# From the sixth group on, q and k come as bf16 blocks by casting DMA and are transposed by DMA

## The chip, the cores and the metric

The kernel runs on one core of one Trainium2 chip. Its time is device time in microseconds; three runs of the kernel before gave 258.83, 259.00 and 259.49 us, a median of 259.0. The profile is of one further execution, whose own time was 260.0 us and whose span from the first to the last instruction was 258.2 us. The TensorE clock was granted in full (1.0).

## The reference

Two layers, one after the other. First block-causal attention over 8 batches, 8 heads, 576 positions and head size 64, in fp32:

```python
scores = scale * np.matmul(q, k.transpose(0, 1, 3, 2))      # scale = 1/8
mask = (pos[:, None] // 64) >= (pos[None, :] // 64)
attn = softmax(np.where(mask, scores, -1e9))
attn_out = np.matmul(attn, v)
```

Then the heads are laid side by side as x, 4608 tokens of 512 features, and go through a maxout layer with 1024 hidden features:

```python
g = np.maximum(x @ w1, x @ w2)
out = g @ w_out
```

## The kernel before, in words

**Algebra of the second layer.** max(a, b) is b + max(a - b, 0). The kernel forms d = w1 - w2 once, computes relu(x d) (`h_unit`, line 202; the relu is line 220) and adds x (w2 w_out) with M = w2 w_out computed once (`m_unit`). An output tile of 128 tokens (`y_unit`, line 252) is 4 matmuls of x with M and 8 of g with w_out.

**Tiling of the attention.** Two heads make a pair, since two heads of 64 fill the 128 partitions; two pairs make a group g. There are 32 pairs and 16 groups (NG), two groups (GPB) to a batch. Everything is computed in transposed form: the scores matmul (`scores`, line 366) needs q and k with the head dimension on the partitions (tiles `qT` and `kT`, one per pair, a ring of four, NT = 4), and so does the second layer with x (`xT`).

**How q and k get there before the change.** `load_qk(g, ...)` (line 112) loads a group's q and k, fp32, by two DMAs on SP's queue into raw tiles (three buffers each; position 9p + t of a head goes to partition p, so that each partition reads one run of 2304 bytes per head). A tiny memset on Pool ahead of each (`gated`) keeps the load from starting too early. `cast` (line 126) turns them into bf16 on Pool, one instruction of 1152 values per partition each. `transposes` (line 346) transposes them on TensorE, 18 matmuls with the identity per q or k of a group into two PSUM tiles, and copies these into `qT` and `kT`, one on DVE, one on ACT (line 360). v is loaded by Pool's casting DMA (`load_v`, line 134), five chunks per batch.

**Softmax and attention times v.** For each pair three PSUM tiles of scores are filled (`tile_0`, `tile_1`, `tile_2`), ACT takes the exponential into `aT` (`exp`, line 395), and Pool zeroes the blocks above the diagonal (`mask`, line 400). `tile_2` has corner blocks whose keys come from `kz`, a copy of some columns of `kT` made on Pool by `pad_keys` (line 377). `av` (line 463), two pairs later (LAG = 2), multiplies with v on TensorE, and DVE divides by the row sums into `xp`.

**x.** For the first four groups and the last, TensorE transposes `xp` into `xT` (`x_out`). For groups 4 to 14 SP does it with two transposing DMAs (`x_dma`, lines 494 to 497), one group later than the scores.

**Order of the work.** The order is written out by hand (`manual_schedule`): each engine executes its instructions in the order in which the Python code emits them. The second layer is a list of units, from which `fill(n)` emits some n matmuls wherever attention would leave TensorE waiting; a unit may be emitted once the tokens it reads are accounted done (`done_tokens`). In the main loop each group of two pairs a and b emits: the scores of a's first two tiles; for a, then for b: fill, `av` of two pairs ago, for b also `x_dma` of the group before, then the transposes of the next group's q (at a) or k (at b) by `t_pair`, further score tiles, the copies out of the transposes, the exps and masks, at b also `pad_keys` for the next group, and last `pool_work` (line 541), which holds Pool's share: loads for the group three ahead, casts for the group two ahead, v for the next batch. SP's queue holds the loads of q and k, the transposes of x and the stores of y, in the order emitted; a store waits there until ACT or DVE has copied its tile out of PSUM.

Of the kernel before, what the change touches and what calls it, by code (L numbers as in the profile page):

```python
# [9 lines left out]
BF16 = mybir.dt.bfloat16  # L10
# [4 lines left out]
def kernel(  # L15
# [10 lines left out]
    nc = tc.nc  # L26

    B, H, S, D = q.shape
    P = 128
    BLK = 64  # L30
# [14 lines left out]
    NG = NPAIR // 2  # L45
    GPB = HP // 2
# [36 lines left out]
    raw = ctx.enter_context(tc.tile_pool(name="raw", bufs=3))  # L83
# [10 lines left out]
    NV, NA, NT = 3, 4, 4  # L94
    qT_r = [ring.tile([P, S], BF16, name=f"qT{r}") for r in range(NT)]
    kz_r = [ring.tile([P, 3 * BLK], BF16, name=f"kz{r}") for r in range(NT)]
    kT_r = [ring.tile([P, S], BF16, name=f"kT{r}") for r in range(NT)]
# [12 lines left out]
    dve, pool, act = nc.vector.tensor_copy, nc.gpsimd.tensor_copy, nc.scalar.copy  # L110

    def load_qk(g, queues, gated=False):
        b, u = divmod(g, GPB)
        for nm, src, queue in (("q", q, queues[0]), ("k", k, queues[1])):
            if queue is None:
                continue
            raws[nm, g] = t = raw.tile([P, 2, RPP * D], FP32, name=f"{nm}raw")
            if gated:
                nc.gpsimd.memset(t[:, 0, :1], 0.0)
            queue.dma_start(  # L120
                out=t[:],
                in_=src[b, 4 * u:4 * u + 4].rearrange(
                    "(s h) (p t) d -> (h p) s (t d)", h=2, t=RPP),
            )

    def cast(nm, g, parts):
        t = raws[nm, g].rearrange("p s (t d) -> p t s d", d=D)
        if (nm, g) not in qk_n:
            qk_n[nm, g] = qkn.tile([P, RPP, 2, D], BF16, name=f"{nm}n")
        n = qk_n[nm, g]  # L130
        for copy, j0, j1 in parts:
            copy(out=n[:, j0:j1], in_=t[:, j0:j1])  # L132

    def load_v(b, c):
        rows = min(P, S - c * P)
        nc.gpsimd.dma_start(  # L136
            out=vv_r[b % NV][P - rows:, c, :, :D],
            in_=v[b, :, c * P:c * P + rows, :].rearrange("h p d -> p h d"),
        )
# [7 lines left out]
    for j in range(d_ff // WB):  # L147
        row, n = (1, j) if j < 3 else (3, 0)
# [22 lines left out]
    dve, pool, act = nc.vector.tensor_copy, nc.gpsimd.tensor_copy, nc.scalar.copy  # L171
# [174 lines left out]
    def transposes(nm, g, copies):  # L346
        n = qk_n.pop((nm, g))
        pts = [ps_m.tile([P, RPP, NP], BF16, name=f"ps_{nm}T", tag="m") for _ in range(2)]
        for j in range(RPP):
            for i in range(2):  # L350
                r = slice(i * NP, (i + 1) * NP)
                nc.tensor.transpose(  # L352
                    pts[i][:, j, :], n[r, j].rearrange("p s d -> p (s d)"), ident[r, r],
                )

        def copy_out(which=(0, 1), part=(0, NP), copy=None):
            p0, p1 = part
            for i in which:
                t = (qT_r if nm == "q" else kT_r)[(2 * g + i) % NT]
                (copy or copies[i])(  # L360
                    out=t[:, p0 * RPP:p1 * RPP].rearrange("q (p j) -> q p j", j=RPP),
                    in_=pts[i][:, :, p0:p1].rearrange("q j p -> q p j"),
                )
        return copy_out
# [67 lines left out]
    def tile_0(p):  # L432
        u = ps_s.tile([P, 2, 512], FP32, name="ps_s", tag="s")
        scores(p, u, 0, 0, 0, 512)
        return lambda: (exp(p, u, 512, 0), mask(p, 0))

    def tile_1(p):
        u = ps_s.tile([P, 2, 512], FP32, name="ps_s", tag="s")
        scores(p, u, 0, 0, 512, 64)
        scores(p, u, 64, 1, 128, 448)  # L440
        return lambda: (exp(p, u, 512, 512), mask(p, 576))

    def tile_2(p):
        u = ps_s.tile([P, 2, 512], FP32, name="ps_s", tag="s")
        corner_scores(p, u, 320)
        scores(p, u, 0, 2, 256, 320)
        scores(p, u, 384, 3, 448, P)

        def out():
            exp(p, u, 512, 1024)  # L450
            nc.scalar.activation(
                out=aT_r[p % NA][BLK:, :, 1536:AW], in_=u[BLK:, :, 320:320 + BLK],
                func=AF.Exp, scale=scale,
            )
            mask(p, 1024)
            mask(p, 1344)
        return out

    def region(*tiles):
        for out in tiles:  # L460
            out()
# [29 lines left out]
    def x_by_dma(g):  # L491
        return BY_DMA <= g < NG - 1

    def x_dma(g):
        b, u = divmod(g, GPB)
        for s in range(2):
            nc.sync.dma_start_transpose(
                out=xT[:, 2 * u + s, b * S:b * S + NCH * P].rearrange(
                    "p (t w) -> p t w", w=P),
                in_=xps[g][:, s].rearrange("p t a d -> p (t a d)"),  # L500
            )

    def x_out(g, t0=0, t1=NCH, copies=(dve, dve)):
        b, u = divmod(g, GPB)
        if x_by_dma(g):
            if u == GPB - 1:
                done_tokens[0] = (b + 1) * S
            return
        xp = xps[g]
        n = t1 - t0  # L510
        n_odd = min(t1, NCH - 1) - t0
        pe = ps_m.tile([P, 2, n, BLK], BF16, name="ps_xe", tag="m")
        po = ps_m.tile([P, 2, n_odd, BLK], BF16, name="ps_xo", tag="m")
        for s in range(2):
            for t in range(t0, t1):
                src = xp[:, s, t].rearrange("p a d -> p (a d)")
                nc.tensor.transpose(pe[:, s, t - t0, :], src[:BLK], ident[:BLK, :BLK])
                if t < NCH - 1:
                    nc.tensor.transpose(po[:, s, t - t0, :], src[BLK:], ident[BLK:, BLK:])
        dst = xT[:, 2 * u:2 * u + 2, b * S + t0 * P:b * S + t1 * P].rearrange(  # L520
            "p s (t h w) -> p s t h w", h=2, w=BLK)
        copies[0](out=dst[:, :, :, 0], in_=pe[:])
        copies[1](out=dst[:, :, :n_odd, 1], in_=po[:])
        if u == GPB - 1:
            done_tokens[0] = min(b * S + t1 * P, (b + 1) * S)
# [8 lines left out]
    def fill_of(g):  # L534
        if g == NG - 1:
            return 45
        left = 5 - g if g < 5 else 2 - (g - 5) % 2
        return -(-max(0, ready() - KEEP) // left)


    def pool_work(s):
        g, i = divmod(s, 2)
        if s == 4:
            load_qk(4, (SP, SP), gated=True)
        elif s == 5:
            load_qk(5, (SP, SP), gated=True)
            cast("q", 4, ((pool, 0, RPP),))
            cast("k", 4, ((pool, 0, RPP),))
        else:
            if i == 1 and g + 3 < NG:  # L550
                load_qk(g + 3, (SP, SP), gated=True)
            if i == 1 and g + 2 < NG:
                cast("q", g + 2, ((pool, 0, RPP),))
                cast("k", g + 2, ((pool, 0, RPP),))
            nb, j = divmod(s + 2, HP)
            if nb < B:
                for c in ((0, 1), (2, 3), (4,), ())[j]:
                    load_v(nb, c)

    T_AT = {s: [("qk"[s % 2], s // 2 + 1)] for s in range(NPAIR - 2)}  # L560
    T_AT[0] = T_AT[1] = T_AT[2] = T_AT[3] = []

    def t_pair(s):
        outs = [transposes(nm, g, (dve, act)) for nm, g in T_AT.get(s, [])]
        return lambda: [f() for f in outs]


# [3 lines left out]
    def av_with(p, n):  # L571
        av(p, [0, 1])
        fill(n)
        av(p, [2, 3, 4])
# [82 lines left out]
    outs = tile_0(4), tile_1(4)  # L657
# [13 lines left out]
    n = fill_of(GPB)  # L671
# [10 lines left out]
    for g in range(GPB + 1, NG):  # L682
        a, b = 2 * g, 2 * g + 1
        old = done_tokens[0]
        if x_due:
            x_out(x_due.pop())
        n, new = fill_of(g), done_tokens[0]
        region(tile_0(a), tile_1(a))
        lo, hi = max(3, n // 18), n * 2 // 9
        for p, tiles in ((a, lambda: (tile_2(a), tile_0(b))), (b, lambda: (tile_1(b), tile_2(b)))):  # L690
            if p == a and x_by_dma(g - 2):
                done_tokens[0] = old
            rest = fill(hi)
            done_tokens[0] = new
            fill(rest)
            av_with(p - LAG, lo)
            if p % 2 and x_by_dma(g - 1):
                x_dma(g - 1)
            copy_out = t_pair(p)
            outs = tiles()  # L700
            copy_out()
            region(*outs)
            if p % 2 and g + 1 < NG:
                pad_keys(p + 1)
                pad_keys(p + 2)
            pool_work(p)
        x_due.append(g - 1)
        fill(n - 2 * (lo + hi))
# [49 lines left out]
```

The softmax here doesn't subtract the row's maximum and nothing guards it: scores larger than these inputs give would overflow.

## Time and profile before

| | |
|---|---|
| median of three runs | 259.0 us |
| profiled execution | 260.0 us, span 258.2 us |
| TensorE (PE) busy | 247.4 us, 96% |
| weight loads (PEld) | 139.1 us, 54% |
| VectorE (DVE) busy | 136.1 us, 53% |
| ScalarE (ACT) busy | 143.2 us, 55% |
| Pool (GpSimd) busy | 110.4 us, 43% |
| transposes of q and k on TensorE (L352) | 2 x 288 matmuls, 7.0 and 7.1 us busy |
| casts of q and k on Pool (L132) | 1.15 us each |
| copies of qT and kT out of PSUM (L360) | 0.64 us on ACT, 0.75 us on DVE each |
| v loads' issue on Pool (L136) | 40 of them, mean 0.85 us |
| transposes of x, issue on SP (L497) | 22 of them, median 1.27 us |

PE is TensorE, PEld its weight loads, DVE VectorE, ACT ScalarE, POOL GpSimd and SP SyncE, which here only issues DMAs. L352 is line 352 of the kernel. Issuing a DMA is not counted as busy, so the time that Pool spends on the v loads stands beside its 43%. DMA packets are listed by queue: q1 is SP's, q0 Pool's; the share given with them adds the packets' own durations, which overlap. Besides the page, the trace's records of single DMA packets (queue, size, start, duration) can be counted in a stretch of time. "Group" in what follows is one round of the main loop.

### The profile page before, as it was taken

The numbers are of one execution on the slowest core, as the hardware profiler recorded it, in microseconds if no ns is written. First come the engines' busy times: TensorE is split into PE (matmuls) and PEld (weight loads), VectorE is DVE, ScalarE is ACT, GpSimd is POOL, SyncE is SP. The second block draws the span as 40 slices with busy tenths as digits, with TensorE's granted clock in tenths as the row PEclk, the third lists the DMA queues.
The fourth block names the chain that finished last, engine by engine and source line by source line (L and its number), as shares of the span: only waits on it lengthen the run. The fifth ranks groups of instructions, "written<-read, shape, count | busy, mean of one in ns | idle before, by whom it ended". The sixth has DMA issues, their size and how long they took to land.

```text
span 258.2 us, 7195 instructions
## 1 busy us (share of the span) xinstructions
PE 247.4 (96%) x2983; PEld 139.1 (54%) x2983; DVE 136.1 (53%) x299; ACT 143.2 (55%) x200; POOL 110.4 (43%) x274
## 2 busy tenths in 40 slices
PE   7598899799999999999999999999999999999995
PEld 2346678646555555555555554546464655444444
DVE  4967986556584428451845184518550853443200
ACT  2798854476574857586757665766576431000111
POOL 1987950584637263726382638163813010000000
PEclk9999999999999999999999999999999999999999
DMA  6999999499569995998599949985977122202122
GB/s 244 316 206 307 217 251 246 156 102 253 129 162 257 144 188 135 245 154 225 114 244 143 186 145 224 168 196 141 91 109 110 44 56 80 83 0 81 43 104 99
DMA packets 71265, 41.30 MB, mean 160 GB/s; under 512 B 53568, under 2 KB 58048, under 8 KB 71232
## 3 DMA queue, kind: packets, MB, share of 16 engines
q1 hardware_dynamic: 28544, 31.27, 43.4%
q0 software_dynamic: 42272, 8.92, 39.9%
q10 hardware_dynamic: 416, 0.66, 0.7%
q8 instruction: 23, 0.38, 0.6%
q14 instruction: 10, 0.08, 0.1%
HBM read 34.60 MB, written 9.44 MB: 171 GB/s over the span
## 4 chain that ended last, share of the span: by engine, by line
PE 84%; DMA 8%; POOL 3%; ACT 2%; issue 1%; DVE 0%; SPq 0%; POOLq 0%; ACTq 0%
PE ps_y L257 36%; PE ps_h L215 22%; PE ps_o L479 10%; PE ps_s L371 8%; DMA qraw<-in_q_dram 5%; DMA kraw<-in_k_dram 3%; PE ps_qT L352 2%; PE ps_kT L352 2%; PE ps_w L341 1%; ACT aT L395 1%; PE ps_y L272 1%; PE ps_M L238 1%; POOL kn L132 1%; PE ps_s L389 1%; ACT qT L360 1%
## 5 line engine op out<-in xcount | busy, mean ns | idle before, releaser
L395 ACT ACTIVATE aT<-ps_s 128x1024 bf16<-128x1024 f32 (+2 forms) x100 | 95.8, 996 | 25.8 <-PE ps_s L371 24.2
L257 PE MATMUL ps_y<-wo_sb,g 128*128 128x512 bf16 x280 | 69.8, 379 | 0.0
L215 PE MATMUL ps_h<-xT,d_sb 128*128 128x512 bf16 (+3 forms) x320 | 69.2, 358 | 0.3 <-DVE d_sb L162 0.3
L220 DVE TENSOR_SCALAR g<-ps_h 128x512 bf16<-128x512 f32 (+3 forms) x80 | 50.7, 636 | 30.6 <-PE ps_h L215 28.8
L400 POOL MEMSET aT<- 64x128 bf16 x124 | 22.4, 200 | 81.8 <-ACT aT L395 81.2
L485 DVE RECIPROCAL rec<-ps_o 128x4 f32<-128x4 f32 (+1 forms) x64 | 12.1, 188 | 62.5 <-PE ps_o L479 61.7
L215 PEld LDWEIGHTS <-d_sb 128*128 128x128 bf16 x320 | 29.0, 98 | 29.1 <-issue 2.7
L479 PEld LDWEIGHTS <-aT 128*128 128x128 bf16 x960 | 37.2, 98 | 13.5 <-issue 0.8
L262 ACT COPY y<-ps_y 128x512 f32<-128x512 f32 x31 | 18.2, 587 | 44.5 <-PE ps_y L257 36.1
L257 PEld LDWEIGHTS <-g 128*128 128x128 bf16 x280 | 25.8, 98 | 29.8 <-issue 2.0
L479 PE MATMUL ps_o<-vv,aT 128*128 128x65 bf16 x960 | 39.8, 194 | 0.0
L257 PE MATMUL ps_y<-m_sb,xT 128*128 128x512 bf16 x140 | 38.2, 380 | 0.0
L136 POOL DMA_DIRECT2D vv<-in_v_dram x40 | 33.7, 848 | 1.6 <-issue 1.2
L371 PE MATMUL ps_s<-qT,kT 64*128 64x64 bf16 (+6 forms) x344 | 31.2, 280 | 1.6 <-ACT kT L360 0.7
L486 DVE TENSOR_TENSOR xp<-ps_o,rec 128x256 bf16<-128x256 f32 (+1 forms) x64 | 31.4, 491 | 2.2
L360 ACT COPY qT<-ps_qT 128x576 bf16<-128x576 bf16 (+1 forms) x17 | 10.3, 614 | 19.9 <-PE ps_qT L352 19.9
L132 POOL CAST qn<-qraw 128x1152 bf16<-128x1152 f32 (+1 forms) x16 | 16.9, 1058 | 9.1 <-DMA qraw<-in_q_dram 9.1
L257 PEld LDWEIGHTS <-xT 128*128 128x128 bf16 x140 | 12.2, 98 | 15.1 <-issue 3.5
L371 PEld LDWEIGHTS <-kT 64*128 64x128 bf16 x344 | 12.3, 94 | 11.0 <-issue 6.2
L132 POOL CAST kn<-kraw 128x1152 bf16<-128x1152 f32 (+1 forms) x15 | 17.1, 1140 | 1.4 <-DMA kraw<-in_k_dram 1.4
L360 ACT COPY kT<-ps_kT 128x576 bf16<-128x576 bf16 x15 | 9.6, 639 | 14.4 <-PE ps_kT L352 14.4
L207 POOL COPY g<-g 128x512 bf16<-128x512 bf16 x8 | 4.9, 614 | 20.7 <-DVE g L220 20.3
(58 smaller groups left out, 161.8 us busy)
## 6 DMA issues: line engine op xcount, KB each, us to landing
qraw<-in_q_dram SPq DMA_DIRECT2D x16, 576.0 KB, 5.0
out_dram<-y SPq DMA_DIRECT2D x35, 256.0 KB, 3.7
kraw<-in_k_dram SPq DMA_DIRECT2D x15, 576.0 KB, 5.8
vv<-in_v_dram POOLq DMA_DIRECT2D x32, 128.0 KB, 5.7
w1raw<-in_moe_w_dram POOLq DMA_DIRECT2D x4, 512.0 KB, 8.1
xT<-in_moe_w_dram POOLq DMA_DIRECT2D x4, 256.0 KB, 8.6
wo_sb<-in_moe_w_out_dram POOLq DMA_DIRECT2D x2, 512.0 KB, 10.0
kraw<-in_k_dram ACTq DMA_DIRECT2D x1, 576.0 KB, 5.6
```

Of the source, the lines that this page charges most:

```text
L132: copy(out=n[:, j0:j1], in_=t[:, j0:j1])
L136: nc.gpsimd.dma_start(out=vv_r[b % NV][P - rows:, c, :, :D], in_=v[b, :, c * P:c * P + rows, :].rearrange("h p d -> p h d"),)
L215: nc.tensor.matmul(pt[:, :w], d_sb[:, c, f * P:(f + 1) * P], xT[:, c, t0:t0 + w], start=(c == 0), stop=(c == NDM - 1),)
L220: nc.vector.tensor_scalar_max(g[:, f, m:m + w], pt[:, :w], 0.0)
L257: nc.tensor.matmul(py[:], lhs, rhs, start=(n == 0), stop=(n == len(terms) - 1),)
L262: (dve if i < 2 else act)(out=y[:], in_=py[:])
L360: (copy or copies[i])(out=t[:, p0 * RPP:p1 * RPP].rearrange("q (p j) -> q p j", j=RPP), in_=pts[i][:, :, p0:p1].rearrange("q j p -> q p j"),)
L371: nc.tensor.matmul(ps[:, hh, col:col + w], kT[r, k0:k0 + P], qT[r, q0:q0 + w], start=True, stop=True,)
L395: nc.scalar.activation(out=aT_r[p % NA][:, :, a0:a0 + w], in_=ps[:, :, :w], func=AF.Exp, scale=scale,)
L400: (eng or nc.gpsimd).memset(aT_r[p % NA][BLK:, :, a0:a0 + BLK], 0.0)
L479: nc.tensor.matmul(po[:, gi, hh, :], a[:, hh, a0:a0 + P], vv[:, c, h0 + 2 * hh, :], start=(mm == 0), stop=(mm == n_mm - 1),)
L486: nc.vector.tensor_mul(xp[:, :, ts[0]:ts[0] + n, p % 2].rearrange("q s t d -> q t s d"), po[:, :, :, :D], rec[:, :n].to_broadcast([P, n, 2 ...
```

## The change

From group 5 on (the sixth), q and k take another way. `load_blocks` issues eight casting DMAs on Pool's queue per group, one per head of q and of k, each reading a head as nine blocks of 64 positions and writing bf16 into 64 partitions of a tile that shares the raw tiles' buffers. `transpose_blocks` issues four transposing DMAs on SP's queue per group, one per pair of q and of k, straight into `qT` and `kT`. The loads of group g + 2 are emitted by `pool_work` for the first pair of group g, ahead of the v loads; the transposes of group g + 1 are emitted in group g after `av` of the first pair. The fp32 loads on SP, their gating memsets, the casts on Pool, the transposes on TensorE and the copies out of PSUM are left out for these groups. Groups 0 to 4 are as before. The work of the second layer and its order are untouched.

```diff
     def load_qk(g, queues, gated=False):
         b, u = divmod(g, GPB)
         for nm, src, queue in (("q", q, queues[0]), ("k", k, queues[1])):
-            if queue is None:
+            if queue is None or by_dma(nm, g):
                 continue
...
+    T_DMA = {nm: 5 for nm in "qk"}
+    blk_n = {}
+
+    def by_dma(nm, g):
+        return g >= T_DMA.get(nm, NG)
+
+    def load_blocks(nm, g):
+        b, u = divmod(g, GPB)
+        blk_n[nm, g] = n = raw.tile([P, S // BLK, 2, D], BF16, name=f"{nm}b", tag=f"{nm}raw")
+        for h in range(2):
+            for s in range(2):
+                nc.gpsimd.dma_start(
+                    out=n[h * BLK:(h + 1) * BLK, :, s],
+                    in_=(q if nm == "q" else k)[b, 4 * u + 2 * s + h].rearrange(
+                        "(j p) d -> p j d", p=BLK),
+                )
+
+    def transpose_blocks(nm, g):
+        n = blk_n.pop((nm, g))
+        for h in range(2):
+            nc.sync.dma_start_transpose(
+                out=(qT_r if nm == "q" else kT_r)[(2 * g + h) % NT].rearrange(
+                    "q (j p) -> q j p", p=BLK),
+                in_=n[h * BLK:(h + 1) * BLK].rearrange("p j s d -> p (j s d)"),
+            )
+
     def cast(nm, g, parts):
+        if by_dma(nm, g):
+            return
...
             if i == 1 and g + 3 < NG:
                 load_qk(g + 3, (SP, SP), gated=True)
+            if i == 0:
+                for nm in "qk":
+                    if g + 2 < NG and by_dma(nm, g + 2):
+                        load_blocks(nm, g + 2)
             if i == 1 and g + 2 < NG:
                 cast("q", g + 2, ((pool, 0, RPP),))
                 cast("k", g + 2, ((pool, 0, RPP),))
...
-        outs = [transposes(nm, g, (dve, act)) for nm, g in T_AT.get(s, [])]
+        outs = [transposes(nm, g, (dve, act)) for nm, g in T_AT.get(s, []) if not by_dma(nm, g)]
...
             if p % 2 and x_by_dma(g - 1):
                 x_dma(g - 1)
+            if p % 2 == 0:
+                for nm in "qk":
+                    if g + 1 < NG and by_dma(nm, g + 1):
+                        transpose_blocks(nm, g + 1)
             copy_out = t_pair(p)
```

## The prediction

> **What bounds the kernel now.** I read the page first: busy times, then the DMA queues.
>
> ```profile
> span 258.2 us, 7195 instructions
> ...
> PE 247.4 (96%) x2983; PEld 139.1 (54%) x2983; DVE 136.1 (53%) x299; ACT 143.2 (55%) x200; POOL 110.4 (43%) x274
> ...
> q1 hardware_dynamic: 28544, 31.27, 43.4%
> q0 software_dynamic: 42272, 8.92, 39.9%
> ```
>
> TensorE is 96% busy; DVE, ACT and Pool are near half. q1 is SP's queue, q0 is Pool's. Next the chain that ended last, in order of time, over one group of the loop:
>
> ```profile
> 157.64 0.54 PE ps_s L371 x6
> ...
> 161.56 0.37 PE ps_qT L352 x18
> 161.93 0.06 PE ps_s L389 x4
> ...
> 165.80 0.37 PE ps_kT L352 x18
> ...
> 170.63 0.54 PE ps_s L371 x6
> 171.17 1.40 PE ps_y L257 x6
> 172.57 0.43 PE ps_h L215 x2
> ```
>
> Columns are start, us, work. From 58 us on the chain is TensorE alone, and one group takes 170.63 - 157.64 = 12.99 us (13.0 in the others too). The two transposes that the change removes stand on it, 0.37 us each. By the starts of their neighbours they cost a little less: 161.50 to 161.77, 0.28 us.
>
> Since the change moves work onto DMA, I then asked for the DMA rate in four stretches (columns: length; busy us of PE, PEld, DVE, ACT, Pool; clock; DMA share; GB/s):
>
> ```profile
> 37.50:39.20 1.70, 1.70 (x29) 1.22 (x28) 1.54 (x3) 0.64 (x1) 1.06 (x3) 1.00 2.42 154
> 144.00:145.00 1.00, 1.00 (x9) 0.31 (x7) 0.00 (x0) 0.01 (x1) 1.00 (x2) 1.00 1.28 213
> 182.50:184.00 1.50, 1.50 (x12) 0.51 (x9) 1.26 (x2) 0.00 (x0) 1.50 (x4) 1.00 1.62 159
> 157.64:170.63 12.99, 12.99 (x166) 7.04 (x168) 4.35 (x11) 9.32 (x13) 6.59 (x18) 1.00 1.08 198
> ```
>
> A share above 1 says that packets overlap, so it is no measure of fullness; rates are. In the first stretch only Pool's v loads run, from a backlog, in packets of 128 B written: 154 GB/s / 128 B = 1200 packets per us, and the packet records agree (2050 in 1.7 us). In the second SP's transposes of x run nearly alone: 768 packets of 256 B in 1 us. In the third both have a backlog: the records count 470 of Pool's and 632 of SP's in 1.5 us, 735 per us together. Three more such stretches (77.5 to 80.5, 129.5 to 131.5, 155.5 to 158.5) give 714, 746 and 711. So Pool's small packets and SP's transposes together run no faster than transposes alone.
>
> Last, SP's and Pool's own order of time:
>
> ```profile
> 161.32 4.79 SPq L263 DMA_DIRECT2D out_dram<-y  x2
> 166.66 2.53 SPq L497 DMA_TRANSPOSE xT<-xp  x2
> ```
>
> ```profile
> 157.90 1.16 POOL L132 CAST kn<-kraw 128x1152 bf16<-128x1152 f32 x1
> 158.99 1.75 POOL L136 DMA_DIRECT2D vv<-in_v_dram  x2
> ...
> 165.27 0.69 POOL L136 DMA_DIRECT2D vv<-in_v_dram  x1
> ```
>
> **What the Trainium skill says.** "DMA: Bandwidth & Descriptors", section "Issuing engines are not separate DMA queues": DMAs of SP, ACT and Pool run on the same 16 engines and interleave. The mixed stretches agree. Its section "Why small descriptors are slow (HBM only)" puts a fixed overhead on every packet. The trace agrees: q1's load packets of 2304 B take 93 ns at the median, Pool's of 128 B 32 ns, 18 times fewer bytes in a third of the time. "VectorE: DVE Perf Modes", section "The three transpose paths", has 390 ns on TensorE and 1309 ns by DMA for a 128x128 block. In this trace SP spends 1268 ns at the median on a transpose of five such blocks, so I use that.
>
> **The change part by part**, for the eleven groups 5 to 15.
>
> *TensorE.* 22 sets of 18 transposes go: 22 x 0.28 = 6.2 us by starts, 22 x 0.37 = 8.1 by the chain. I take the middle, 7.1; the group becomes about 12.35 us.
>
> *ACT, DVE.* 22 copies each out of PSUM go (0.64 us on ACT, 0.75 on DVE). Neither sets the group, so this is worth nothing by itself; the exps, and so the masks, come some 0.6 us earlier.
>
> *Pool.* The casts (two of 1.15 us) and two gating memsets (0.2) go, 2.5 us per group; eight loads come, each 64 x 9 runs of 64 values, 576 packets. The v load with 512 packets holds Pool 0.69 us, the one with 1024 0.88: I take 0.71, eight are 5.7 us. Net +3.2 us; Pool has 6.4 us idle in the group shown. The loads stand between the masks of a pair's first tiles and those of its last, with the copies into kz behind. Moving the block that began at 152.61 on with its two v loads: 152.6 + 5.7 + 1.75 = 160.1, masks 0.6, kz 0.5: 161.2, against corner scores due at 161.77 less 0.65 for the faster group. With ACT's 0.6 us it just fits. Any added wait on a load (in the built program each Pool DMA waits for the eighth before it) comes through to TensorE there.
>
> *SP.* Two loads (0.4 us each) go, four transposes come. Each reads 576 rows of 256 B where one of x reads 640: 1268 x 576 / 640 = 1.14 us, four 4.6 us. This form is not in the trace; if the cost goes by blocks of 128 columns (nine against five) it is 2.3 us, four 9.1. I take 1.14. Behind them in SP's order stand y's store, and then x's pair.
>
> *DMA engines.* Per group, mean over a batch's two: Pool 8 x 576 = 4608 packets new, v (4 x 1024 + 512) / 2 = 2304 as before; SP 4 x 576 = 2304 new, x 2 x 640 = 1280 as before; y some 256 to 300 packets of 84 ns; the 512 packets of 2304 B go. Priced with the rates above:
> - SP's 3584 transposed packets, mixed, at some 385 per us: 9.3 us, in which about 340 per us of Pool's pass, 3170.
> - Pool's other 3740 at 1200: 3.1 us.
> - y: 295 x 84 / 16 = 1.55 us.
> - Sum 14.0 us. With the isolated rate of Pool's pairs (53 to 56 us: 1989 in 3 us) for the rest it is 16.5; with no mixing, 3584 / 768 + 6912 / 1200 + 1.55 = 12.0.
>
> The same sum for the kernel before: 1280 / 385 = 3.3, the other 1170 of v 1.0, loads 512 x 93 / 16 = 3.0, y 1.55: 8.9 of 13.0 us, hidden with room. After, 14.0 against TensorE's 12.35: the DMA engines set the group.
>
> *What is late next.* Loads are issued a group before their transposes, and these most of a group before the scores, so early lateness is absorbed; then Pool stalls on its eighth-back DMA, with masks and kz behind, or x's pair lands late. Groups 4 to 13 have both parts: 10 x (14.0 - 13.0) = +10; group 14 has only transposes, -0.65. Span 258.2 + 9.4 = 267.6. The profiled execution took 260.0, 1.8 us around its span, and stands 1.0 above the median 259.0; so the median is span + 0.8: **268.4, say 268**.
>
> **The rivals.**
>
> *All hidden, faster.* Transposes and loads start at different times of a group (SP near its fourth us, Pool near its eighth) and mix little. If the mean rate is above (6912 + 3584) / (12.35 - 1.55) = 970 packets per us, between the mixed 725 and the pure 1200, TensorE stays the bound: 258.2 - 7.1 + 0.8 = 252, with a us for leftovers 253. For it: no engine but TensorE is near full. Against: SP is issuing 7.2 of 12.35 us (4.6 and x's 2.6) and Pool's loads stream for most of the group, so they must overlap.
>
> *Only x is late.* When a batch ends, its x pair (issued 166.66, last packet 170.1) is needed by the first ps_h at 172.57, 2.4 us later. After, it runs inside the new burst. Pairs that met v packets landed up to 3.2 us later than clean ones (3.45 us from first issue; 6.6 at the worst). A loss of 1 to 3 us in about four groups takes back 4 to 12 of the 7: 254 to 264, about 259.
>
> *SP or Pool bound.* At 2.3 us per transpose SP issues 9.1 + 2.6 + 1 = 12.7 us per group and x's pair starts some 4 us later than it may; or the loads cost 0.88 us and their waits add up on Pool. 2 to 3 us over 13.0 in ten groups: 278 to 288.
>
> *That it does not do what it says* is excluded: the built program has 792 fewer TensorE rows, 88 casting loads and 44 transposes on SP.
>
> **How the numbers follow.** DMA engines as the bound 0.42 (260 to 284 by itself), all hidden 0.22, only x late 0.18 (of it 0.05 faster, 0.06 same, 0.07 slower), SP or Pool bound 0.18. Within 0.3% is about what a measurement tells from no change. Faster 0.22 + 0.05 = 0.27; same 0.06; slower 0.42 + 0.07 + 0.18 = 0.67. Range 252.5 to 286: it takes in most of the hidden case and the mixed rate down to 15.8 us per group, and leaves out a cleaner success and the upper part of the SP case.
>
> **What would show it.** Right: the start-to-start of groups near 14 us where both parts run; packets near 725 per us for most of the group; kz (L406) or Pool's loads (L137) waiting for DMA, and TensorE idle before scores or ps_h. The TensorE step is right if ps_qT and ps_kT fall from 288 matmuls each to 90; the Pool step if L137 is near 0.71 us; the SP step if L146 is near 1.14. Wrong if groups are 12.4 us and TensorE still 96% busy (hidden), if idle time stands only before the first ps_h of a batch (x late), or if SP or Pool issues without a gap while the DMA rate is low.

## The result and the profile after

The changed kernel took 288.05 us (median of four executions, 286.13 to 289.4) where the kernel before took 259.12 in the same comparison: 1.111 times as long, 95% interval 1.1033 to 1.1187. The forecast was 268 with a range of 252.5 to 286. The sign was right, the size was too small by 20 us, and the time lies above the range. Ratios here and below leave disturbed executions out, so for four kernels (`q_only`, `unread`, `turn_late` and `turn_late_dve`) they lie below the ratio of the medians.

The profiled execution took 289.4 us. Its page, with the busy times, the row of the granted TensorE clock (tenths, 40 slices) and the two DMA queues:

```profile
span 287.6 us, 6494 instructions
...
PE 255.8 (89%) x2587; PEld 138.6 (48%) x2587; DVE 121.8 (42%) x277; ACT 131.3 (46%) x178; POOL 149.8 (52%) x318
...
PEclk9999999999599968999799979997799999999999
...
q0 software_dynamic: 94368, 15.41, 78.2%
q1 hardware_dynamic: 49312, 24.78, 43.0%
```

TensorE has 396 instructions fewer than before (2983 - 2587, the 2 x 198 transposes taken out), and yet is busy 8.4 us longer, because its clock is no longer granted in full. Pool's queue carries 94368 packets instead of 42272, SP's 49312 instead of 28544, for the same bytes (41.25 MB in all, 41.30 before).

In the lines of the changed kernel, L137 is the new loads, L146 the new transposes, L164 the loads of v, L243 the matmuls of x with d, L399 the scores, L406 the copies into `kz`, L507 attention times v and L525 the transposes of x; in the kernels of the experiments they can lie some lines off.

The waits (us in all, times, longest), of TensorE and of Pool's copies into `kz`:

```profile
PE ps_h L243 <- DMA xT<-xp: 13.8, 8, 3.4
...
POOL kz L406 <- DMA kT<-kb: 6.5, 5, 2.6
...
PE ps_s L399 <- DMA kT<-kb: 4.8, 4, 2.2
...
PE ps_o L507 <- DMA vv<-in_v_dram: 3.5, 1, 3.5
```

None of these four waits is in the kernel before. The largest is not for q and k, which the change moved, but for x, which it did not touch. The chain that ended last shows it too (start, us, work):

```profile
159.97 1.29 SPq L525
161.32 6.95 DMA xT<-xp
168.30 1.01 PE ps_h L243 x2
```

In the kernel before this stretch of the chain was TensorE alone. Now it leaves TensorE for SP's issue of x's second transpose and 6.95 us of its transfer.

From the starts of each group's first scores, groups 5 to 14 took 18.67, 12.47, 18.89, 13.31, 18.21, 13.59, 17.95, 14.75, 18.51 and 13.23 us, 15.96 in the mean, against 13.0 before. Ten times 2.96 is 29.6, which is the whole loss of span (287.6 - 258.2 = 29.4). So a short group and a long one take turns, with the two groups of a batch. One such pair, by windows (length; busy us of PE, PEld, DVE, ACT, Pool; clock; DMA share; GB/s), and then two parts of the long group:

```profile
147.80:161.39 13.59, 12.53 (x129) 6.54 (x129) 3.08 (x9) 8.22 (x11) 11.90 (x24) 1.00 1.98 147
161.39:179.34 17.95, 14.04 (x129) 7.38 (x130) 7.64 (x16) 7.01 (x9) 8.02 (x20) 0.90 1.22 150
...
164.01:167.38 3.37, 0.01 (x1) 0.00 (x0) 0.61 (x2) 0.35 (x1) 1.25 (x4) 1.00 1.72 165
167.70:171.10 3.40, 2.86 (x37) 2.00 (x35) 1.08 (x3) 0.00 (x0) 0.00 (x0) 0.50 1.21 282
```

For 3.37 us TensorE does nothing, and then it runs for 3.4 us at a clock of 0.50. The order of time of SP, of Pool and of TensorE (start, us, work; in brackets the idle time before it and what ended it) shows what it waited for:

```profile
152.04 2.92 SPq L146 DMA_TRANSPOSE qT<-qb  x2
155.12 4.13 SPq L146 DMA_TRANSPOSE kT<-kb  x2
159.35 0.52 SPq L291 DMA_DIRECT2D out_dram<-y  x1
159.97 2.72 SPq L525 DMA_TRANSPOSE xT<-xp  x2
```

```profile
155.21 2.93 POOL L137 DMA_DIRECT2D qb<-in_q_dram  x4 [0.32 <-issue]
158.10 2.96 POOL L137 DMA_DIRECT2D kb<-in_k_dram  x4
160.97 0.78 POOL L164 DMA_DIRECT2D vv<-in_v_dram  x1
```

```profile
161.39 0.61 PE L399 MATMUL ps_s<-qT,kT 64*128 64x512 bf16 x6 [1.06 <-DMA kT<-kb]
...
163.67 0.34 PE L507 MATMUL ps_o<-vv,aT 128*128 128x65 bf16 x6
167.38 0.38 PE L243 MATMUL ps_h<-xT,d_sb 128*128 128x512 bf16 x1 [3.37 <-DMA xT<-xp]
```

From 155.2 to 161.1 Pool issues the eight loads, 4608 packets. In the same time SP issues k's transposes and then x's pair. TensorE stands at 164.01, when the x pair issued from 159.97 on has not landed. The packet records say why: from 160.0 to 163.5 us the engines wrote 2769 of Pool's packets and only 581 of SP's transposing ones, 166 per us of these, where x's pair alone is 1280. The load of v's fifth chunk stands behind the loads of q and k in Pool's order, at 160.97, and lands at 167.95.

### The profile page after: what moved, and what is told of

Same layout as the page of the kernel before. It is cut to its first block, busy times and chain, and to the rows that moved or that the text cites. A ratio compares the mean times of both kernels' runs of the same rounds, so it can differ in the third digit from the quotient of the medians.

```text
span 287.6 us, 6494 instructions
## 1 busy us (share of the span) xinstructions
PE 255.8 (89%) x2587; PEld 138.6 (48%) x2587; DVE 121.8 (42%) x277; ACT 131.3 (46%) x178; POOL 149.8 (52%) x318
## 2 busy tenths in 40 slices
DMA packets 144125, 41.25 MB, mean 143 GB/s; under 512 B 132064, under 2 KB 136544, under 8 KB 144096
## 3 DMA queue, kind: packets, MB, share of 16 engines
q0 software_dynamic: 94368, 15.41, 78.2%
q1 hardware_dynamic: 49312, 24.78, 43.0%
## 4 chain that ended last, share of the span: by engine, by line
PE 62%; DMA 19%; POOL 8%; ACT 5%; issue 2%; SPq 2%; DVE 1%; ACTq 0%; POOLq 0%
PE ps_y L285 22%; PE ps_h L243 20%; DMA xT<-xp 10%; PE ps_o L507 8%; PE ps_s L399 6%; PE ps_w L369 3%; DMA kraw<-in_k_dram 3%; ACT aT L423 3%; DMA qraw<-in_q_dram 2%; POOL qb L137 2%; POOL kb L137 2%; DMA kT<-kb 2%; SPq L525 2%; DMA vv<-in_v_dram 2%; PE ps_s L417 1%
## 5 line engine op out<-in xcount | busy, mean ns | idle before, releaser
L243 PE MATMUL ps_h<-xT,d_sb 128*128 128x512 bf16 (+3 forms) x320 | 75.1, 378 | 14.2 <-DMA xT<-xp 13.8
L285 PE MATMUL ps_y<-wo_sb,g 128*128 128x512 bf16 x280 | 70.8, 383 | 0.0
L243 PEld LDWEIGHTS <-d_sb 128*128 128x128 bf16 x320 | 30.4, 101 | 48.0 <-issue 24.5
L507 PEld LDWEIGHTS <-aT 128*128 128x128 bf16 x960 | 40.1, 102 | 18.4 <-issue 6.4
L507 PE MATMUL ps_o<-vv,aT 128*128 128x65 bf16 x960 | 42.8, 200 | 3.5 <-DMA vv<-in_v_dram 3.5
L399 PE MATMUL ps_s<-qT,kT 64*128 64x64 bf16 (+6 forms) x344 | 33.1, 294 | 6.3 <-DMA kT<-kb 4.8
L164 POOL DMA_DIRECT2D vv<-in_v_dram x40 | 34.7, 885 | 0.7 <-DMA qb<-in_q_dram 0.5
L137 POOL DMA_DIRECT2D qb<-in_q_dram x44 | 32.2, 747 | 3.0 <-issue 2.8
L137 POOL DMA_DIRECT2D kb<-in_k_dram x44 | 32.6, 787 | 0.5 <-DMA vv<-in_v_dram 0.5
L399 PEld LDWEIGHTS <-kT 64*128 64x128 bf16 x344 | 12.6, 98 | 17.1 <-DMA kT<-kb 6.7
L285 PEld LDWEIGHTS <-xT 128*128 128x128 bf16 x140 | 12.2, 98 | 15.1 <-issue 3.5
L406 POOL COPY kz<-kT 128x128 bf16<-128x128 bf16 x28 | 8.2, 317 | 10.2 <-DMA kT<-kb 6.5
L369 PE MATMUL ps_w<-zeros 128*128 128x512 bf16 x29 | 10.4, 504 | 2.4 <-DVE zeros L205 1.2
```

The source lines that it names most:

```text
L137: nc.gpsimd.dma_start(out=n[h * BLK:(h + 1) * BLK, :, s], in_=(q if nm == "q" else k)[b, 4 * u + 2 * s + h].rearrange("(j p) d -> p j d", ...
L164: nc.gpsimd.dma_start(out=vv_r[b % NV][P - rows:, c, :, :D], in_=v[b, :, c * P:c * P + rows, :].rearrange("h p d -> p h d"),)
L243: nc.tensor.matmul(pt[:, :w], d_sb[:, c, f * P:(f + 1) * P], xT[:, c, t0:t0 + w], start=(c == 0), stop=(c == NDM - 1),)
L285: nc.tensor.matmul(py[:], lhs, rhs, start=(n == 0), stop=(n == len(terms) - 1),)
L369: nc.tensor.matmul(pw[:], zeros[:, :P], zeros[:], start=True, stop=True)
L399: nc.tensor.matmul(ps[:, hh, col:col + w], kT[r, k0:k0 + P], qT[r, q0:q0 + w], start=True, stop=True,)
```

## The experiments

Rates and idle shares of the DMA engines come from the trace's packet records, group lengths from the starts of the first 64x512 scores of each group. The engines are called nearly idle in a quarter of a us in which fewer than ten packets begin, counted over groups 5 to 14. First the two theories: the engines have no room (14.0 us per group, as forecast), or single items are late behind the burst of loads.

**The loads half a group earlier, at the end of a group instead of in the middle of the next** (`moved`). Those for group 5 are issued with the casts for group 4.

```diff
+            load_blocks("q", 5)
+            load_blocks("k", 5)
...
             if i == 1 and g + 3 < NG:
                 load_qk(g + 3, (SP, SP), gated=True)
-            if i == 0:
                 for nm in "qk":
-                    if g + 2 < NG and by_dma(nm, g + 2):
-                        load_blocks(nm, g + 2)
+                    if by_dma(nm, g + 3):
+                        load_blocks(nm, g + 3)
```

> The eight loads of a group are issued half a group earlier in the round before (by the second pair, for the group three ahead, after kz), so that they no longer start just before x's pair of transposes. DMA work unchanged. If the packets of a group fill the DMA engines (the prediction): no gain, 283 to 290 us. If x's pair is late because it runs inside the burst of loads: the odd groups fall from 18 to about 12.5 us, 252 to 262 us in all.

It took 280.93 us, 1.0855 times before (1.0791 to 1.092). Long and short groups no longer take turns: the first of the ten is 19.0, the last 12.5, and those between are 14.1 to 16.9. TensorE now waits 12.6 us for `kT` and 4.8 for `xT`, and the engines are nearly idle in 5% of the quarters of a us, against 11% in the changed kernel. The result lies between what the two theories foresaw: the place of the burst was worth 7 us, and the rest did not go with it.

**x's pair not needed so soon** (`keep24`: `KEEP`, the number of units left over for the next group, from 6 to 24).

> KEEP = 24 for 6: 18 more matmuls of older work, some 4 us, are held back to run before the first matmul that needs the new xT. DMA and queues unchanged. If the DMA engines are full: no gain, 285 to 290 us. If only the wait for xT costs, with the slow clock after it: most of the 5 to 6 us in each of four groups comes back, 262 to 272 us.

It took 295.41 us (1.1407, 1.1364 to 1.1451), longer than with the wait. TensorE no longer waits for x. Its wait is now the first of these lines; then Pool's and TensorE's order of time:

```profile
PE ps_o L507 <- DMA vv<-in_v_dram: 28.0, 5, 6.7
```

```profile
160.11 2.97 POOL L137 DMA_DIRECT2D kb<-in_k_dram  x4
164.72 0.69 POOL L164 DMA_DIRECT2D vv<-in_v_dram  x1 [1.64 <-DMA qb<-in_q_dram]
```

```profile
172.83 0.49 PE L507 MATMUL ps_o<-vv,aT 128*128 128x65 bf16 x6 [6.74 <-DMA vv<-in_v_dram]
```

Pool issues v's fifth chunk behind the eight loads, after a wait for an earlier load, and it lands some 8 us later. In the changed kernel this lateness is there too (v lands at 167.95 us in the group shown), but the wait for x, which comes ahead of it and ends at 168.30, covers it. So two items are late together, and taking the wait for x away alone brings out the one for v; v's chunk taken away alone was not run. Part of the added 7 us is this edit's own cost, as `before_early` below shows.

**Only the loads, or only the transposes.** In `loads_only` the blocks come by Pool's casting DMA and TensorE transposes them as before. In `transposes_only` SP's DMA transposes a fixed tile of zeros into `qT` and `kT`, and q and k of groups 5 to 15 are not loaded.

```diff
 # loads_only
-        n = qk_n.pop((nm, g))
+        n = blk_n.pop((nm, g)) if by_dma(nm, g) else qk_n.pop((nm, g))
...
+                if by_dma(nm, g):
+                    copies[i](out=t.rearrange("q (j p) -> q j p", p=NP), in_=pts[i][:])
+                    continue
 # transposes_only
-        n = blk_n.pop((nm, g))
+        n = still
```

> The loads by Pool as in the change, the transposes on TensorE again (copies out of PSUM too). If the DMA engines are full only with both parts: 9.7 us of DMA per group, about 259 to 262 us. If x's pair is late because of the burst of loads alone: stalls remain, 272 to 290 us. If it is late because it stands behind the four transposes on SP: about 259 us.

> The four transposes on SP as in the change, but from one fixed tile of zeros; q and k of groups 5 to 15 are not loaded at all, so the output leaves them out. If the burst of loads makes x late, or fills the engines: about 252 to 254 us. If x is late because it stands behind the transposes on SP: 268 to 285 us.

The loads alone took 277.31 us (1.0725, 1.0663 to 1.0786), and their two largest DMA waits in TensorE are the two items:

```profile
PE ps_o L510 <- DMA vv<-in_v_dram: 5.6, 4, 1.7
PE ps_h L243 <- DMA xT<-xp: 5.3, 6, 2.5
```

They also tell which of the two new streams makes x late. In group 10 of the kernel before, x's pair is issued 9.1 us after the group's start, and both have landed 4.8 us after the first issue. With the loads alone it is issued at 9.1 too and takes 8.5 us; with the transposes alone it is issued at 10.8, behind them on SP, takes 3.9 us, and TensorE doesn't wait for it. So the burst of loads is what slows it, and its later place on SP's queue is not enough by itself.

The transposes alone took 254.53 us (0.9836, 0.9796 to 0.9875), with eight of the ten groups at 12.46 to 12.47 us. This is the gain on TensorE as it would be with everything else hidden, 13.0 - 12.47 = 0.53 us per group.

**Both late items taken away**, with both parts (`both_early`) and with the loads alone (`loads_early`): `KEEP` is 24, and v's fifth chunk is issued with its third and fourth, ahead of the burst.

```diff
-    KEEP = 6
+    KEEP = 24
...
-                for c in ((0, 1), (2, 3), (4,), ())[j]:
+                for c in ((0, 1), (2, 3, 4), (), ())[j]:
```

> The change with the two late items given room at once: KEEP = 24, and v's fifth chunk loaded half a group before the burst of loads instead of behind it. DMA work unchanged. If those two waits are the whole loss: groups of about 12.5 us, 252 to 262 us. If the DMA engines need 14 to 16 us per group for these packets, as the run with the loads moved suggests (14.7 us per group, engines hardly ever idle): 270 to 285 us, with the waits turning up elsewhere.

> Pool's loads alone (transposes on TensorE), with KEEP = 24 and v's fifth chunk ahead of the burst. By the sum of packets this needs 9.7 us of DMA per group against 13.0, so both theories say about 258 to 262 us: the 18 us of the loads alone were two late items, not engines without room. Above 268 us the burst would cost in a third way.

They took 272.14 (1.0536, 1.0478 to 1.0595) and 265.04 us (1.0238, 1.0197 to 1.0279). In the first, TensorE's waits for v are gone, those for x are down to 1.7 us, and the largest that is left is the chain of load, transpose and scores:

```profile
PE ps_s L399 <- DMA kT<-kb: 7.7, 3, 3.1
POOL kb L137 <- DMA vv<-in_v_dram: 6.8, 6, 2.3
```

The second line is Pool waiting, before it issues a load, for an earlier DMA to end. The engines are nearly idle in 0.5% of the quarters of a us.

**The same two edits on the kernel before** (`before_early`), to know what they are worth by themselves.

> The kernel before with the same two edits of order: x's pair not needed for 24 units, v's fifth chunk with the third and fourth. TensorE is never idle in its groups now, so nothing is to be gained: 258 to 260 us. If it comes out 2 us or more apart from the kernel before, the runs with these edits have to be read against it instead.

264.58 us (1.0199, 1.0161 to 1.0237): the edits cost 5.5 us, where nothing was expected. Two places of it in TensorE's order of time:

```profile
47.83 0.44 PE L352 MATMUL ps_qT<-ident,qn 64*128 64x64 bf16 x18 [2.15 <-POOL qn L132]
...
100.45 0.90 PE L479 MATMUL ps_o<-vv,aT 128*128 128x65 bf16 x24 [0.43 <-ACT y L262]
```

The units that are held back leave TensorE idle while the first groups still wait for their casts (with a stretch of half clock at 49.0), and the odd groups are 13.58 us instead of 13.0. So `both_early` and `loads_early` must be read against 264.6 (and `keep24`, which has one of the two edits, at least in part). Then the loads alone, with nothing late behind them, cost 0.5 us, which the two intervals can't tell from nothing; and the whole change costs 7.6. Had this been left out, all 13 us of `both_early` would have been put down to the engines.

**Long runs instead of many packets** (`long_runs`): the kernel before, with q and k of groups 5 to 15 loaded by Pool's casting DMA in the old layout, 512 packets per group instead of 4608; casts, transposes and copies stay as before.

```diff
-            raws[nm, g] = t = raw.tile([P, 2, RPP * D], FP32, name=f"{nm}raw")
+            raws[nm, g] = t = raw.tile([P, 2, RPP * D], BF16 if g >= 5 else FP32,
+                                       name=f"{nm}raw", tag=f"{nm}raw")
...
-            queue.dma_start(
+            (nc.gpsimd if g >= 5 else queue).dma_start(
```

> The kernel before, but q and k of groups 5 to 15 come by Pool's casting DMA in the old layout: 2304 bytes read per run, 512 packets per group instead of 4608, the same bytes; the copy on Pool stays, now bf16 to bf16. If the number of packets makes the loads dear: 256 to 262 us. If it is Pool's queue or the cast as such: 268 us or more, like the loads alone (277).

258.63 us, 0.9975 (0.9955 to 0.9994). So neither Pool's queue nor the cast in the DMA makes the loads dear by itself. What is left is the block layout, which makes nine packets out of one. It was not isolated: these loads are also emitted half a group earlier than those of `loads_only`, and are two DMAs per group instead of eight. The Trainium skill ("DMA: Bandwidth & Descriptors", section "Why small descriptors are slow (HBM only)") says that each packet has its own overhead, and this pair of runs (258.63 us here, 277.31 in `loads_only`) agrees.

**Nothing waits for the loads** (`unread`): `both_early`, with the loads running but the transposes reading a fixed tile of zeros, so that q and k of groups 5 to 15 are not used.

```diff
-        n = blk_n.pop((nm, g))
+        n = still
```

> As the run with both waits given room (272 us), but the four transposes read a fixed tile of zeros: the loads of q and k still run, in the same number, and nobody reads them, so the output leaves q and k of groups 5 to 15 out. If what remains of the loss is a chain, late loads, then late transposes, then late scores: 254 to 259 us. If it is the engines' room, 735 packets per us for 10500 packets and y's stores in each group: 266 to 273 us, kT late all the same.

The median was 269.9 us (ratio 1.0344, 1.0325 to 1.0363). The profiled execution took 273.9 us, so its waits are read for their kind alone:

```profile
POOL kb L137 <- DMA vv<-in_v_dram: 10.5, 9, 1.7
...
PE ps_s L419 <- POOL kz L408: 6.2, 5, 2.0
PE ps_o L509 <- DMA vv<-in_v_dram: 4.9, 4, 1.7
```

With the chain from load to score cut, Pool waits for its own earlier DMAs, and `kz` and v come late. By the ratios `both_early` is 8.7 us above `before_early` (1.0536 against 1.0199, of 259; 7.6 by the medians) and so 12.9 above what it would be with the 4.2 us of the transposes' gain (0.9836). This kernel is 3.8 above `before_early` (1.0344), so 8.0 of the 12.9 stay where nothing waits for the loads, somewhat more than half, with 0.5 to 1.5 us of uncertainty in each ratio. I put these 8.0 down to the engines' room and the rest to the chain. That is argued, not shown: Pool's order, in which a load waits for an earlier DMA, is in the 8.0 too, and no run takes the two apart.

**q alone** (`q_only`), and q alone with the late items taken away (`q_early`): `T_DMA = {"q": 5}`.

> Only q takes the new way (T_DMA for q alone); k as before. Four loads and two transposes per group. DMA by the prices of the prediction 11.4 us per group, TensorE 12.7. If the engines' room is the cause, and not every burst: 255 to 258 us. If any burst ahead of x's pair costs in proportion: 266 to 274 us.

> Only q by the new way, k as before, with x's pair not needed for 24 units and v's fifth chunk issued with its third and fourth. Account of packets: (2304 of q + 2304 of v + 1152 + 1280 of SP) / 734 = 9.6 us, y's 1.55 and k's 256 long ones 256 x 93 / 16 = 1.5, together 12.6 us against TensorE's 12.7 per group: the engines are just not the bound, groups of 12.7 to 13.1, 256 to 260 us. If the rest of the loss is something that comes with any of the new transposes or loads (a wait of the load, transpose, score chain), it is 264 us or more as with q alone before.

267.25 us (1.0236, 1.0189 to 1.0283) and 260.08 (1.0044, 1.0004 to 1.0083). In the first TensorE waits 4.6 us for x and, in group 5, 2.8 for v. In the second the groups are 12.73 and 13.03 by turns, TensorE's own times, and the engines are nearly idle in 8% of the quarters of a us. Half of the new packets are hidden in full, as the account of packets has it (12.6 us per group), and the run lies 4.5 us below `before_early`.

**A smaller edit, made only from group 5 on** (`q_keep12`, `both_keep12`), with v's fifth chunk early as above.

```diff
-        return -(-max(0, ready() - KEEP) // left)
+        return -(-max(0, ready() - (KEEP if g < 5 else 12)) // left)
```

> q alone by the new way; units of x's pair not needed for 12 units instead of 24, and only from group 5 on; v's fifth chunk with the third and fourth. The 2.6 us ahead of group 5 come back, and the odd groups' extra 0.3 us mostly: groups of 12.73 to 12.9, about 256 to 257.5 us, below the kernel before. If 12 units are too few to cover x's pair, which was up to 1.2 us late with 6, there are waits for x again: 258 to 262 us.

> The whole change with the same two edits. If the engines' room sets the group once nothing stands behind the burst, groups stay at 13.5 to 14 us and the time falls only by what is given back ahead of group 5 and in the odd groups: 267 to 271 us. If the earlier 272 us was mostly the cost of the edit itself, it comes to 262 to 266. If x's pair is late again, TensorE waits for x: above 274 us.

With q alone it took 257.82 us, 0.996 times the kernel before (0.9945 to 0.9976): the fastest whole computation here, 1.0 us below it. Its page:

```profile
span 255.8 us, 6799 instructions
...
PE 241.1 (94%) x2751; PEld 136.2 (53%) x2785; DVE 129.3 (51%) x288; ACT 136.2 (53%) x189; POOL 130.2 (51%) x296
```

With q and k it took 269.26 (1.0426, 1.0385 to 1.0466), and what TensorE waits for is k's chain:

```profile
PE ps_s L399 <- DMA kT<-kb: 6.8, 3, 3.5
...
PE ps_h L243 <- DMA xT<-xp: 1.5, 3, 0.8
```

Groups 5 to 14 take (202.78 - 65.18) / 10 = 13.76 us, at 759 packets of both kinds per us in the mean, and the engines are nearly idle in 1% of the time. Most groups are 12.5 to 13.3; three of 15.1 to 17.0 give the rest, one of them with a stretch of half clock behind it. Group 6 moved 11643 packets of both kinds in 12.52 us (930 per us), more than a group's share of 10496.

**Long runs and transposes by DMA together.** If few packets make the loads cheap and the transposes gain 4 us, both should beat `q_keep12`. q and k are loaded and cast on Pool as before; SP transposes the cast tile into a spare tile, and copies put the columns in order into `qT` and `kT`. In `turn_long` the copies stand on DVE and ACT ahead of the second pair's exps, in `turn_late` after them, in `turn_late_dve` after them and all on DVE. `turn_ahead` issues casts and transposes earlier; `turn_calm` puts the casts back and makes the two edits of `both_early`.

```diff
+            turned[nm, g, h] = t = tt.tile([P, S], BF16, name=f"{nm}x{h}", tag=f"{nm}x{h}")
+            nc.sync.dma_start_transpose(
+                out=t.rearrange("q (j p) -> q j p", p=NP),
+                in_=n[h * NP:(h + 1) * NP].rearrange("p j s d -> p (j s d)"),
+            )
...
+                (dve, act)[h](
+                    out=t.rearrange("q (p j) -> q p j", j=RPP),
+                    in_=turned.pop((nm, g, h)).rearrange("q (j p) -> q p j", p=NP),
+                )
```

> A version that keeps the gain and leaves the small packets: q and k come as in the kernel before (long runs on SP, cast on Pool), SP's transposing DMA turns the cast tile of groups 5 to 15 into a spare tile at the start of the group before, and DVE and ACT copy that into qT and kT in the order of positions, as they copied from PSUM. TensorE loses the same 22 sets of transposes; DMA per group by the prices of the prediction 3584 / 385 = 9.3 us with v inside, loads 3.0, y 1.55: 13.9 us if v always mixes, 12.4 if only half of it does. If TensorE stays the bound, as in the run with transposes alone: 252.5 to 255 us. If these transposes meet the loads on the engines: 257 to 264 us.

> The long-run loads and the transposes by DMA of the spare-tile kernel, with the copies into qT and kT (pair a's on DVE, pair b's on ACT) emitted after the second pair's exps instead of ahead of them. If that kernel lost its time only because ACT's copies stood waiting for a transpose ahead of the exps, TensorE is the bound again at 12.4 to 12.7 us per group: 253 to 257 us. If the copies are still late for the next group's scores (ACT does its four exps and then two copies of 1.2 us, and the corner copies kz on Pool wait for them), TensorE waits for ACT's kT before the first scores of the second pair or for kz: groups of 13 to 14.5 us, 260 to 278 us. If the DMA engines are the limit even with few load packets, the time stays above 280.

> As the other, but all four copies on DVE (0.68 us each by the run before, 2.7 us per group), after the second pair's exps in the order of emission. DVE has no exps in front of them, so they can run as soon as the transposes have landed, some 9 us after the group's start: 253 to 256 us with groups of 12.4 to 12.6 us if ACT's order was the whole cause. If DVE's share of the second layer's evictions is held up behind copies that wait, TensorE waits for PSUM tiles of h or y: groups of 13 to 14 us, 260 to 270 us.

> As the spare-tile kernel with all copies on DVE, but the casts of group g + 2 are emitted for the first pair of group g and its transposes at the end of group g, ahead of the gated loads, so that they should land some 4 us into the next group, 5 us ahead of the copies. If the long groups left were only the loop of late copies, late gates and late transposes, all groups from 5 on are 12.4 to 12.6 us as with the transposes alone: 253 to 256 us. If the engines have no room for transposes and v's packets at the same time, two or three groups stay at 14 to 18 us: 259 to 268 us.

> Long load runs and transposes by DMA into spare tiles, copies on DVE; the casts go back behind the second pair's exps, where their loads have long landed, with the transposes right behind them; x's pair isn't needed for 24 units, and v's fifth chunk is issued with its third and fourth. If the long groups of the last form came only from v and x, all groups from 5 on are 12.4 to 12.6 us and the kernel takes 253 to 256 us, below the kernel before. If the engines have no room for it, groups of 13 us and more stay: 258 us or more.

They took 287.19 (1.108, 1.1045 to 1.1114), 272.22 (1.0464, 1.0381 to 1.0548), 263.51 (1.0143, 1.0083 to 1.0203), 268.95 (1.0406, 1.0382 to 1.0429) and 270.12 us (1.0423, 1.0393 to 1.0453). The first fell because ACT, in order, stood 32.5 us waiting for a transpose ahead of the exps. In the second TensorE waits 8.8 us in all for DVE's copies into `kT`. The third (its profiled execution took 267.3 us) reaches 12.46 to 12.48 us in six of the ten groups from 5 on, the full gain, and loses it in the others. Two of the places, in group 4, where the first spare tiles are copied, and in group 11, where DVE's evictions stand behind the copies:

```profile
68.40 1.04 PE L392 MATMUL ps_s<-qT,kT 64*128 64x512 bf16 x6 [3.72 <-DVE kT L150]
...
163.26 1.01 PE L278 MATMUL ps_y<-m_sb,xT 128*128 128x512 bf16 x2 [3.74 <-DVE g L241]
```

In the fourth the even groups are all 12.46 to 12.47, but Pool's earlier casts wait for their loads, with v's chunks behind them, and TensorE waits for v and x again in the odd ones:

```profile
POOL qn L132 <- DMA qraw<-in_q_dram: 37.1, 13, 5.0
```

The fifth, which has the 5.5 us of `before_early` in it, waits for `kz` and the copies. No form here held the full gain. Four full-gain groups in a row in the third show that the engines can carry few load packets and all the transposes; an order that holds it throughout was not found.

## Why the prediction was wrong, step by step

- **TensorE's saving, 7.1 us (6.2 by starts, 8.1 by the chain).** Right in kind: 90 rows each of the q and k transposes are left. In size the starts were the better view: 0.53 us per group and 11 groups are 5.8. The whole run with the transposes alone gained 4.3 (258.80 - 254.53).
- **Pool, 0.71 us per load.** The trace has 0.75 (q) and 0.78 (k) at the median, below. Nearly right, and `kz` did become late, 6.5 us in all.

```profile
L137 POOL DMA_DIRECT2D qb<-in_q_dram x44: 727/746/772, 50.5 to 208.9; - x44
L137 POOL DMA_DIRECT2D kb<-in_k_dram x44: 734/784/817, 53.5 to 211.8; - x44
```

- **SP, 1.14 us per transpose, with 2.3 as the other end.** Measured 1.22 to 1.23 at the median; the longest 2.4. The low end was the right one. Its 576 rows cost hardly less than x's 640 (1.30 now, 1.27 before), so the scaling by rows took off too much.
- **The DMA engines, 14.0 us per group, +10 in all.** The size came out once nothing stands behind the burst: 13.76 us in `both_keep12`, and 269.26 us against the 268 forecast. But the kernel as changed is not that kernel, and the agreement is in part luck. The 13.76 is a mean of even groups and a few long ones, not a steady 14, and part of it is the chain. The rate under the sum, some 725 per us for a mixture, is no ceiling either: the changed kernel moved 957 per us from 160.0 to 163.5 us (2769 and 581 packets), and group 6 of `both_keep12` 930 per us.
- **"What is late next": "early lateness is absorbed; then Pool stalls ..., with masks and kz behind, or x's pair lands late".** This is the step that failed. It named x's pair but gave it no term in the sum, and x's lateness alone was made a rival that excludes the engines' bound (1 to 3 us in about four groups). In the run it comes on top: x's pair is late in groups 7, 9, 11 and 13, by up to 3.4 us at once. Behind it is v's fifth chunk, which the prediction did not see: TensorE waits 3.5 us for it in group 5, and up to 6.7 in `keep24`, where the wait for x is gone. The loads of a later group were emitted ahead of that chunk on Pool's queue, and the chunk is due within the next group. The mean rate was reckoned over a group, while the two items meet the burst at its densest, when SP's transposes get 166 packets per us instead of the 385 that I took for a mixture.
- **No term for the clock.** The Trainium skill ("TensorE: Matmul & The Clock Gate", section "What's actually happening") says that TensorE falls to half its clock after an idle window of some 3.4 us. The sum had idle time in it and no price for what follows. The trace agrees in kind: in the changed kernel's groups 5 to 14 the clock was 0.5 for 27.3 us, in six stretches, which costs up to 13.7 us of work (the last section has idle times below 3.4 us).
- **The sum.** From `both_keep12` (269.3) to the changed kernel (288.05), 18.7 us go with the late items and the clock behind them, and from the kernel before to `both_keep12` some 10.5 net with the engines' room and the chain. Only the second was in the forecast.

**The rivals.** *All hidden* is false for the whole change, true for half of it: `q_early`. *Only x is late* had the right item in the wrong place, as a cause beside the engines' bound and not on top of it. *SP or Pool bound*, 278 to 288, has nearly the time, but not for its reason: its transposes of 2.3 us and loads of 0.88 are not there, and Pool worked 11.90 of 13.59 us in a short group but only 8.02 of 17.95 in a long one. These figures, like the 43% of the kernel before, have Pool's DMA issues in them (the changed kernel's page lists 32.2 and 32.6 us of busy time for L137 and 34.7 for L164); the remark ahead of the prediction that the time of the v loads stands beside the 43% is wrong.

What stays open is how the 10.5 us divide between the engines' room, Pool's order and the chain (`unread` leaves somewhat more than half to the first two), and how the 18.7 divide between idle time and half clock.

## What to carry to other kernels

Before a burst of DMAs is put into a queue, list what stands behind it in that queue and what shares its engines, with the time at which each is needed: a mean rate that fits the group says nothing of an item that is due in 3 us. When a wait is taken away and the time doesn't fall, look for a second item that was late under it; and make the edit that takes the wait away on the kernel before as well, since here it cost 5.5 us of its own. A layout that a transfer needs is paid in packets: with nine for each run of 2304 bytes, a load that cost nothing in `long_runs` cost 18.5 us in `loads_only` (277.31 against 258.80), where other transfers stood behind it, and 0.5 us in `loads_early`, where none did.

## What the runs showed of the hardware that was not expected

- SP's transposes and Pool's small packets don't share evenly. While Pool's queue had a full burst, transposing packets fell to 166 per us (160.0 to 163.5 us: 2769 of Pool's, 581 of SP's); just after the burst had begun (156 to 158 us) it was 322 of Pool's and 462 of SP's per us.
- The clock fell around idle times shorter than the skill's 3.4 us. In `turn_ahead` TensorE was idle from 180.63 to 182.69, 2.06 us, with 0.53 and 0.20 us shortly before, and the clock was at half for 6.8 us from 181.71 on, while the idle time still ran. In the changed kernel idle times of 2.62 and 1.28 us (from 132.22 and 135.21) came before 3.4 us at half clock. Others of 2.4 and 3.1 us had none with them (`both_early`, at 90.58; `moved`, at 98.09), so the length of one idle time doesn't decide it; what does is not shown. The stretches were 3.4 or 6.8 us long, in all the kernels here, where the end of the program didn't cut them.
